# Two more key blocks as 16-bit parts, with their lower halves made by GpSimd

## The chip, the cores and the metric

The kernel runs on one core of a Trainium2 chip. The time is device time in microseconds (us), and the figure compared is the median of several runs. The engines are TensorE (PE, with its weight loads shown apart as PEld), VectorE (DVE), ScalarE (ACT), GpSimd (POOL) and SyncE (SP), which mostly issues DMAs. Each engine works through its own queue in order and waits on semaphores for the others.

## The reference

The input x has 2048 rows of 640 numbers. The result is the sum of x, an attention block and an MLP block, both on the normalised rows:

```
xn = layernorm(x)
q, k, v = split(xn @ wqkv)               # 32 heads of 20 numbers
p = softmax(q @ k.T * 20**-0.5)          # for each head: 2048 x 2048
attention = (p @ v) @ wo
y = layernorm(xn)
mlp = gelu(y @ w1 + b1) @ w2 + b2        # 640 -> 1536 -> 640
out = x + attention + mlp
```

All of it is in 32-bit floats.

## The kernel before, in words

The kernel has three stages. In the first (up to about 236 us) the rows are normalised and transposed, and q, k and v are made. In the last (from about 1272 us) the remaining output projection is done. In between lies the attention stage, and the MLP's matmuls are laid into it as filling.

**The attention loop** (lines 1200 to 1227). It goes over pairs of heads `g`, halves of the queries `hf` and quarters `cc` (512 queries each): 16 x 2 x 2 = 64 accumulations. Each has 16 key blocks `kb` of 128 keys, in four groups of four (`GRP = 4`). For each key block, `scores` (line 742) multiplies two heads' keys and queries into a PSUM tile of 128x1024 (two heads by 512 queries), and ACT writes the exponential of it as 32-bit floats into a tile `p` (line 750). There are seven `p` tiles.

**Split and whole blocks.** The table `SPLIT` (line 27) says how a block enters the second product, p times v. A *whole* block goes into TensorE as 32-bit floats (`vfull`, 32-bit v). A *split* block goes as two 16-bit parts: the upper half of each 32-bit word, read in place as a bfloat16 with a step of two (`upper`, line 753), and the remainder p minus upper, rounded to float16 (`low`, made by DVE on line 762 into a tile of its own, of which there are four). For split blocks v lies as two float16 parts too. Before, `SPLIT` is `(1, 1, 0, 0)` repeated: the first two blocks of each group are split, eight of the 16.

**The second product** (`pv`, line 767) is issued for a whole group at once, one group late: at the last step of the following group. Its results go to one PSUM tile `o`, whose 128 rows are four quarters of 32 (`q`, line 779): a product writes one quarter, so products to different quarters use different columns of the array. A split block has four products with the upper part (two heads by two parts of v, quarters 0 to 3) and two with the lower part; a whole block has two, in 32 bits. The lower products alternate between two quarters of a head:

```
for a in range(2):
    for n, (kb, _, low) in enumerate(split):
        product(2 * a + n % 2, vhalf, of16(kb, a), low[:, a])
```

**The order of a group.** After blocks 0 and 1 of a group have been scored, `rest` (line 757) makes the lower half of block 0, and then a piece of the filling is issued (`other`: MLP or projection matmuls, as many as a running credit of cost allows). After blocks 2 and 3, `rest` is called for the others, and `pv` of the previous group is issued. So DVE has two subtractions per group, one at each step. Beside them DVE does the GELU arithmetic of the MLP (lines 966 to 981), the evictions of the MLP's second layer (line 997) and the normalisation of finished heads (lines 950 to 956).

**GpSimd's queue** in this stage holds only 16 DMAs (line 1051), which add the bias b2 to rows that SP has loaded (line 1050) after SP has stored the rows before (line 1002). After the main loop it makes a selection matrix (line 887).

There is also a path for unusual inputs (`general`, line 1256), which does not run here; it puts the two parts of v together again.

Of the kernel before, what the change touches and what calls it, by code (L numbers as in the profile page):

```python
# [10 lines left out]
F16 = mybir.dt.float16  # L11
# [3 lines left out]
ALU = mybir.AluOpType  # L15
# [3 lines left out]
P = 128  # L19
S, D, H, DH, F = 2048, 640, 32, 20, 1536  # L20
KD = D // P
KF = F // P
NKB = S // P
VW = DH + 1
PAD = 32 - VW
VROW = H * VW + PAD
SPLIT = (1, 1, 0, 0) * (NKB // 4)
NPAIR = H // 2
EPS = 1e-5
TOP = 15.5  # L30
# [3 lines left out]
GRP = 4  # L34
# [10 lines left out]
def mha_mlp_kernel(tc, x, wqkv, wo, w1, b1, w2, b2, out):  # L45
    nc = tc.nc
# [3 lines left out]
    with (  # L50
# [124 lines left out]
        with tc.tile_pool(name="pa", bufs=2) as pa, tc.tile_pool(name="pa1", bufs=1) as pa1, tc.manual_schedule():  # L175
# [33 lines left out]
            for kb in range(NKB):  # L209
                if SPLIT[kb]:  # L210
                    nc.gpsimd.memset(V16[:, kb, :, DH : DH + 1], 1.0)
# [341 lines left out]
            pt = [pts[0][:, 0], pts[0][:, 1], pts[1][:, 0], pts[1][:, 1]]  # L553
# [114 lines left out]
        with ExitStack() as scope:  # L668
# [3 lines left out]
            ptp = pool(name="pt", bufs=2 * GRP - 1)  # L672
# [80 lines left out]
            def upper(pt):  # L753

                return pt.bitcast(BF16).rearrange("p a (n t) -> p a n t", t=2)[:, :, :, 1]

            def rest(unit):

                kb, pt = unit[3:]
                if SPLIT[kb]:  # L760
                    low = ptp.tile([P, 2, 512], F16, tag="low", name="low", bufs=GRP)
                    nc.vector.tensor_sub(low, pt, upper(pt))  # L762
                    unit.append(low)

            evs = {}
# [410 lines left out]
            with tc.manual_schedule():  # L1176
                fill = chain()
                sides.append(fetch_sums())
                credit = 0.0 - next(fill)
                rate = 1.265  # L1180
                groups = [(g, hf, cc, kb) for g, hf in ORDER for cc in range(2) for kb in range(0, NKB, GRP)]
                prev = None

                runs = []

                def other():

                    nonlocal credit
                    if not runs:
                        unit = next(fill)  # L1190
                        if unit is None:
                            credit = 0.0
                            return
                        n, cost = unit
                        k = max(round((cost - credit) / rate) + 1, math.ceil(cost / CHUNK))
                        runs.extend(n * (i + 1) // k - n * i // k for i in range(k))
                    for _ in range(runs.pop(0)):
                        credit -= next(fill)

                for g, hf, cc, kb0 in groups:  # L1200
                    units = []
                    for kb in range(kb0, kb0 + GRP):
                        units.append([g, hf, cc, kb, scores(g, hf, cc, kb)])
                        if kb % 2 == 0:
                            continue
                        reading[0] = kb % GRP > 1 and prev is not None and prev[-1][3] == NKB - 1
                        tick()
                        if kb % GRP == 1:

                            rest(units[0])
                            credit += rate
                            other()
                        else:
                            for u in units[1:]:
                                rest(u)
                            if prev:
                                pv(prev)
                            else:  # L1220

                                credit += rate
                                other()
                    prev = units
                    if cc == 0 and kb0 == 0 and (g, hf) != ORDER[-1]:
                        n = ORDER[ORDER.index((g, hf)) + 1]
                        sides.append(load_stack(*n, *([stacks[g, hf][1]] if n[0] == g else [])))
                n = 0
                reading[0] = False
                ended[0] = True  # L1230
                fetch_results()

                def more(k):
                    nonlocal n
                    for _ in range(k):
                        n += 1
                        cost = next(fill, 0)
                        if isinstance(cost, tuple):
                            cost = next(fill)
                        tick()  # L1240
                        if cost == 0:
                            return False
                    return True

                more(2)
                pv(prev)
                while more(1):
                    pass
                while sides or patient:
                    tick()  # L1250
                flag = nc.values_load(badi, min_val=0, max_val=1)
# [4 lines left out]
def general(tc, nc, V, vscr, qkscr, oscr, accscr, gscale, ident, psS, psO, psM, project):  # L1256


    ds = bass.ds
    nc.sync.dma_start(vscr, V)  # L1260

    assert SPLIT == (1, 1, 0, 0) * (NKB // 4)
    with (
        tc.tile_pool(name="g2", bufs=2) as g2,
        tc.For_i(0, S, P) as t,
    ):
        with tc.For_i(0, D, DH) as r:
            qs = g2.tile([60, P], F16, name="gq")
            ks = g2.tile([60, S], F16, name="gk")
            vr = g2.tile([P, NKB, VW], F32, name="gv")  # L1270
            vt = g2.tile([P, NKB, DH], F32, name="gvt")
            nc.sync.dma_start(qs[: 2 * DH], qkscr[:, ds(r, DH), ds(t, P)])
            nc.sync.dma_start(qs[2 * DH :], qkscr[0, ds(r, DH), ds(t, P)])
            nc.sync.dma_start(ks[:DH], qkscr[0, ds(r + D, DH), :])
            nc.sync.dma_start(ks[DH:], qkscr[:, ds(r + D, DH), :])
            nc.sync.dma_start(vr, vscr[:, :, ds((r // DH) * VW, VW)])
            vp = vr.bitcast(F16)
            for b in range(2):
                nc.vector.tensor_add(vt[:, b::4, :], vp[:, b::4, :DH], vp[:, b::4, VW : VW + DH])
            sf = g2.tile([P, S], F32, tag="sf", name="sf")  # L1280
            m = g2.tile([P, 4], F32, tag="gm", name="gm")
            L = g2.tile([P, 1], F32, tag="gL", name="gL")
            for i in range(2):
                ps = psS.tile([P, 2, 512], F32, tag="s", name="gs")
                for c in range(2):
                    kc = 2 * i + c
                    nc.tensor.matmul(ps[:, c, :], qs, ks[:, kc * 512 : (kc + 1) * 512], start=True, stop=True)
                nc.vector.tensor_copy(sf[:, i * 1024 : (i + 1) * 1024],
                                      ps.rearrange("p a b -> p (a b)"))
            nc.vector.tensor_reduce(m[:, 0:1], sf, AX.X, ALU.max)  # L1290
            nc.vector.tensor_scalar(sf, sf, m[:, 0:1], None, ALU.subtract)
            nc.scalar.activation(sf, sf, AF.Exp, scale=gscale, accum_out=L)
            nc.vector.reciprocal(L, L)
            nc.vector.tensor_scalar(sf, sf, L, None, ALU.mult)
            o = psO.tile([P, 512], F32, tag="o", name="go")
            for kq in range(4):
                pt = psM.tile([P, 512], F32, tag="m", name="gt")
                tt = g2.tile([P, 512], F32, tag="tt", name="tt")
                kb0 = 4 * kq
                for i in range(4):  # L1300
                    nc.tensor.transpose(pt[:, i * P : (i + 1) * P], sf[:, (kb0 + i) * P :][:, :P], ident)
                nc.vector.tensor_copy(tt, pt)
                for i in range(4):
                    nc.tensor.matmul(o[:DH, :P], (vt if SPLIT[kb0 + i] else vr)[:, kb0 + i, :DH], tt[:, i * P : (i + 1) * P],
                                     start=(kb0 + i == 0), stop=(kb0 + i == NKB - 1))
            hl = g2.tile([DH, 2, P], F16, tag="ghl", name="ghl")
            nc.scalar.activation(hl[:, 0], o[:DH, :P], AF.Copy)
            nc.vector.tensor_sub(hl[:, 1], o[:DH, :P], hl[:, 0])
            nc.sync.dma_start(oscr[:, ds(r, DH), ds(t, P)].rearrange("s d t -> d s t"), hl)
        ot = g2.tile([P, KD, 2, P], F16, tag="ot", name="ot")  # L1310
        for s in range(2):
            nc.sync.dma_start(ot[:, :, s, :], oscr[s, :, ds(t, P)].rearrange("(k p) t -> p k t", p=P))
        acc = g2.tile([P, D], F32, tag="acc", name="acc")
        nc.sync.dma_start(acc, accscr[ds(t, P), :])
        project(ot, acc, ds(t, P))
# [27 lines left out]
```

## Time and profile before

| what | value |
|---|---|
| three runs | 1343.22, 1332.72, 1340.56 us (median 1340.56) |
| span of the profiled execution, first to last instruction | 1337.9 us |
| the profiled execution's own time beside its span | not given by the page; the runs lie on both sides of the span |
| mean granted TensorE clock | 0.997 |
| attention stage | about 236 to 1272 us |

The page of the profile gives busy time and its share of the span for each engine, then the chain of work that ended last, then groups of instructions. A group's row reads: line, engine, operation, what it writes and reads, shapes, count; then busy us and the mean length of one in ns; then the engine's idle time just before these instructions and what ended it. A busy share is a mean over the three stages, so the stage that a change touches has to be looked at by itself.

### The profile page before, as it was taken

How to read it: one execution, taken by the hardware profiler on the slowest of the kernel's cores; microseconds unless marked ns; L12 is line 12 of the kernel's file. 1: busy time of each engine (PE TensorE's matmuls, PEld its weight loads, DVE VectorE, ACT ScalarE, POOL GpSimd, SP SyncE). 2: the span in 40 equal slices, each digit the busy share in tenths (PEclk: the TensorE clock that was granted, in tenths of full speed). 3: DMA queues.
4: the chain of work that ended last, by engine and by line, in shares of the span. 5: the costliest groups of instructions: out<-in, count | busy, mean ns of one | idle time of the engine just before them, and what ended most of it. 6: DMA issues, size and time to landing. Idle time of an engine off the chain costs nothing.

```text
span 1337.9 us, 29042 instructions
## 1 busy us (share of the span) xinstructions
PE 1325.8 (99%) x11635; PEld 586.7 (44%) x11635; DVE 1055.1 (79%) x1431; ACT 1128.0 (84%) x1306; POOL 37.5 (3%) x86
## 2 busy tenths in 40 slices
PE   9999899999999999999999999999999999999998
PEld 6645456444434343434343443344443434333366
DVE  7656754998788989878897879888879888997742
ACT  7844334999999999999999999999999999999900
POOL 3010000000000000000000000000000000000000
PEclk9999899999999999999999999999999999999999
DMA  9778723021203232212322132223032323334375
GB/s 279 254 196 176 136 79 104 15 59 39 66 28 103 61 83 81 63 48 59 111 63 81 33 93 66 75 69 94 19 80 71 93 66 87 118 95 118 105 218 188
DMA packets 100326, 129.54 MB, mean 97 GB/s; under 512 B 24292, under 2 KB 66664, under 8 KB 100188
## 3 DMA queue, kind: packets, MB, share of 16 engines
q1 hardware_dynamic: 96652, 120.25, 31.6%
q0 software_dynamic: 2912, 6.90, 2.8%
q8 instruction: 92, 1.51, 0.5%
q10 hardware_dynamic: 624, 0.51, 0.1%
q14 instruction: 46, 0.38, 0.1%
HBM read 82.14 MB, written 42.51 MB: 93 GB/s over the span
## 4 chain that ended last, share of the span: by engine, by line
PE 87%; DVE 6%; DMA 4%; ACT 1%; issue 1%; SPq 0%; ACTq 0%; DVEq 0%
PE o L779 30%; PE s L748 20%; PE py L1061 13%; PE pu L1031 11%; PE z L1146 5%; PE qkp L337 5%; PE vp L410 3%; DVE low L762 2%; DMA xt<-in_A_x_dram 1%; DMA xnt<-row 1%; DMA qkscr<-qkhl 1%; DVE st L255 1%; DVE qkhl L353 1%; ACT p L750 1%; DMA wos<-in_A_wo_dram 0%
## 5 line engine op out<-in xcount | busy, mean ns | idle before, releaser
L750 ACT ACTIVATE p<-s 128x1024 f32<-128x1024 f32 x1024 | 973.9, 1050 | 33.1 <-PE s L748 27.1
L762 DVE TENSOR_TENSOR low<-p 128x1024 f16<-128x1024 f32 x512 | 614.3, 1218 | 144.8 <-ACT p L750 144.0
L779 PE MATMUL o<-p,vfull 128*32 128x512 bf16 (+1 forms) x4096 | 429.0, 493 | 0.0
L748 PE MATMUL s<-qs,ks 61*128 61x512 f16 x2048 | 311.4, 381 | 0.2 <-ACT p L750 0.2
L748 PEld LDWEIGHTS <-ks 61*128 61x128 f16 x2048 | 61.2, 94 | 278.4 <-issue 276.1
L1061 PE MATMUL py<-w2t,hT 128*128 128x320 f16 x1152 | 178.5, 300 | 0.0
L1031 PE MATMUL pu<-xm,w1t 128*128 128x256 f16 x1440 | 178.2, 273 | 0.1
L1031 PEld LDWEIGHTS <-w1t 128*128 128x128 f16 x1440 | 131.0, 98 | 64.0 <-issue 50.2
L1061 PEld LDWEIGHTS <-hT 128*128 128x128 f16 x1152 | 102.3, 98 | 88.1 <-issue 53.9
L337 PE MATMUL qkp<-xnt,wv 128*128 128x512 f16 x600 | 131.1, 379 | 1.3 <-issue 1.3
L779 PEld LDWEIGHTS <-vfull 128*32 128x32 f16 x3072 | 59.9, 95 | 138.4 <-issue 106.9
L779 PE MATMUL o<-low,vfull 128*32 128x512 f16 x1024 | 101.3, 377 | 0.1
L337 PEld LDWEIGHTS <-wv 128*128 128x128 f16 x600 | 58.2, 98 | 71.0 <-issue 1.6
L779 PEld LDWEIGHTS o<-p,vfull 128*32 128x32 f32 x2048 | 61.7, 108 | 53.2
L410 PE MATMUL vp<-wv,xnt 128*128 128x320 f16 x480 | 69.5, 306 | 3.7 <-DVE qkhl L353 3.7
L1146 PE MATMUL z<-w1t,ot 128*128 128x320 f16 x480 | 67.4, 299 | 0.0
L352 ACT ACTIVATE qkhl<-qkp,qks 128x1024 f16<-128x1024 f32 (+1 forms) x24 | 23.1, 964 | 46.3 <-PE qkp L337 26.6
L410 PEld LDWEIGHTS <-xnt 128*128 128x128 f16 x480 | 47.9, 100 | 23.8 <-issue 3.7
L1146 PEld LDWEIGHTS <-ot 128*128 128x128 f16 x480 | 46.0, 98 | 22.9 <-issue 5.5
L353 DVE SCALAR_TENSOR_TENSOR qkhl<-qkp,qks,qkhl 128x1024 f16<-128x1024 f32 (+1 forms) x24 | 26.5, 1104 | 32.9 <-ACT qkhl L352 32.9
L1103 DVE SCALAR_TENSOR_TENSOR acc<-z,sc,acc 128x320 f32<-128x320 f32 x32 | 17.5, 549 | 37.3 <-PE z L1146 37.2
L800 ACT ACTIVATE ev<-o 128x512 f32<-128x512 f32 x64 | 39.5, 618 | 2.2 <-PE o L779 2.1
(195 smaller groups left out, 670.4 us busy)
## 6 DMA issues: line engine op xcount, KB each, us to landing
qkscr<-qkhl SPq DMA_DIRECT2D x40, 256.0 KB
opart<-ev SPq DMA_DIRECT2D x124, 80.0 KB
ks<-qkscr SPq DMA_DIRECT2D x120, 80.0 KB
qs<-qkscr SPq DMA_DIRECT2D x192, 40.0 KB
oa<-opart SPq DMA_DIRECT2D x32, 240.0 KB
xt<-in_A_x_dram SPq DMA_DIRECT2D x16, 320.0 KB
xscr<-xnt SPq DMA_DIRECT2D x4, 1280.0 KB
xm<-xscr SPq DMA_DIRECT2D x8, 640.0 KB
```

Source lines behind the costliest of these rows:

```text
L337: nc.tensor.matmul(ps[:, i, :], wv[:, k, q, a, mm * P : (mm + 1) * P], xnts[c][:, k, b, :], start=(k + n == 0), stop=(k == KD - 1 and n == 2))
L352: nc.scalar.activation(hl[:, 0, i0:i1], ps[:, i0:i1], AF.Copy, scale=a)
L353: nc.vector.scalar_tensor_tensor(hl[:, 1, i0:i1], ps[:, i0:i1], a, hl[:, 0, i0:i1], ALU.mult, ALU.subtract)
L410: nc.tensor.matmul(ps[:, hf, :320], xnts[c][:, k, a, j * P : (j + 1) * P], wv[:, k, 2, b, hf * 320 : (hf + 1) * 320], start=(n == 0), stop ...
L748: nc.tensor.matmul(ps[:, a, :], ks[64 * a : 64 * a + 61, kb * P : (kb + 1) * P], qs[64 * a : 64 * a + 61, cc * 512 : (cc + 1) * 512], star ...
L750: nc.scalar.activation(pt, ps, AF.Exp, scale=QS)
L762: nc.vector.tensor_sub(low, pt, upper(pt))
L779: nc.tensor.matmul(pv.o[32 * q : 32 * q + 32, :], src[:, v0 - PAD * (1 - q % 2) :][:, :32], t, start=q not in pv.begun, stop=last, skip_gr ...
L800: nc.scalar.activation(evs[g, hf][:, cc], pv.o, AF.Copy)
L1031: nc.tensor.matmul(ps[:, i], w1v[:, k, (f + i) // 4, a, fo_ : fo_ + P], xnt[:, k, b, :], start=(n == 0), stop=(n == 3 * KD - 1))
L1061: nc.tensor.matmul(ps[:, :320], hTs[mc][:, f, a, j * P : (j + 1) * P], w2v[:, f, b, hf * 320 : (hf + 1) * 320], start=(n == 0), stop=(n == ...
L1146: nc.tensor.matmul(ps[:, :320], ot[:, k, a, j * P : (j + 1) * P], wov[:, k, b, h * 320 : (h + 1) * 320], start=(n == 0), stop=(n == 3 * KD ...
```

## The change

Ten of the 16 key blocks are split instead of eight. The two more are in the second group of each accumulation (blocks 4 to 7), which becomes wholly split. In that group GpSimd makes the lower halves of blocks 4 and 5, and DVE those of 6 and 7. GpSimd writes in place: the float16 goes into the lower 16 bits of the same 32-bit word of `p`, so no `low` tile is used and the upper halves stay where they are. At the first step of the group both GpSimd subtractions are issued (and the filling), at the second step the two of DVE. The other three groups are as before. Blocks 6 and 7 now have v in two 16-bit parts.

```diff
-SPLIT = (1, 1, 0, 0) * (NKB // 4)
+SPLIT = (1, 1, 0, 0, 1, 1, 1, 1) + (1, 1, 0, 0) * 2
+POOLED = (4, 5)
...
                 kb, pt = unit[3:]
                 if SPLIT[kb]:
-                    low = ptp.tile([P, 2, 512], F16, tag="low", name="low", bufs=GRP)
-                    nc.vector.tensor_sub(low, pt, upper(pt))
+                    if kb in POOLED:
+                        low = pt.bitcast(F16).rearrange("p a (n t) -> p a n t", t=2)[:, :, :, 0]
+                        nc.gpsimd.tensor_tensor(low, pt, upper(pt), ALU.subtract)
+                    else:
+                        low = ptp.tile([P, 2, 512], F16, tag="low", name="low", bufs=GRP)
+                        nc.vector.tensor_sub(low, pt, upper(pt))
                     unit.append(low)
...
-                        if kb % GRP == 1:
-
-
-
+                        if kb in POOLED:
+                            for u in units:
+                                rest(u)
+                            credit += rate
+                            other()
+                        elif kb % GRP == 1:
                             rest(units[0])
                             credit += rate
                             other()
                         else:
-                            for u in units[1:]:
-                                rest(u)
+                            for u in units:
+                                if len(u) == 5:
+                                    rest(u)
```

In `general` the parts of v are put together for every split block instead of every fourth from 0 and from 1.

More of the change, by code (lines that the diff above doesn't have):

```diff
@@ L1260, in general @@
     nc.sync.dma_start(vscr, V)
-    assert SPLIT == (1, 1, 0, 0) * (NKB // 4)
     with (
@@ L1277, in general @@
             vp = vr.bitcast(F16)
-            for b in range(2):
-                nc.vector.tensor_add(vt[:, b::4, :], vp[:, b::4, :DH], vp[:, b::4, VW : VW + DH])
+            for b in range(NKB):
+                if SPLIT[b]:
+                    nc.vector.tensor_add(vt[:, b, :], vp[:, b, :DH], vp[:, b, VW : VW + DH])
             sf = g2.tile([P, S], F32, tag="sf", name="sf")
```

## The prediction

> **What bounds the kernel now.** I read the page first (busy shares, then the chain that ended last), then the busy time of the attention stage by itself, then who waits for whom, and last the order of time on TensorE inside one group of key blocks.
>
> ```profile
> span 1337.9 us, 29042 instructions
> ...
> PE 1325.8 (99%) x11635; PEld 586.7 (44%) x11635; DVE 1055.1 (79%) x1431; ACT 1128.0 (84%) x1306; POOL 37.5 (3%) x86
> ...
> PE 87%; DVE 6%; DMA 4%; ACT 1%; issue 1%; SPq 0%; ACTq 0%; DVEq 0%
> ```
>
> TensorE (PE) is busy 99% of the span and carries 87% of the chain. GpSimd (POOL) does almost nothing. That is a mean over stages, and the change sits only in the attention stage, which the rows of the exp on line 750 place between about 236 and 1272 us. The view of busy time by stretch gives that stage and its tightest 50 us (columns: stretch, length, then busy us and instruction count of PE, PEld, DVE, ACT, POOL; granted clock; DMA share; GB/s):
>
> ```profile
> 236.00:1272.00 1036.00, 1035.59 (x9705) 414.18 (x9697) 885.59 (x1056) 1003.12 (x1125) 13.58 (x16) 1.00 0.26 72
> 250.00:300.00 50.00, 49.76 (x476) 21.41 (x474) 48.49 (x59) 48.78 (x58) 0.00 (x0) 1.00 0.17 47
> ```
>
> So in 1036 us PE has no idle time, ACT has 33 us, and DVE has 150 us (85.5% busy). The stage holds 64 accumulations of 16 key blocks, so one takes 1036 / 64 = 16.19 us, of which DVE works 13.84. The second row shows that DVE can reach 48.49 / 50 = 97% while PE still runs full. Three engines are thus near their limits at once: whoever is given more work has little room. The waits say the same of the order: exp waits for scores, and the subtraction waits for exp.
>
> ```profile
> DVE low L762 <- ACT p L750: 144.0, 121, 8.2
> ...
> ACT p L750 <- PE s L748: 27.1, 110, 0.7
> ```
>
> **What the change takes off TensorE.** Per accumulation two key blocks go from whole (32-bit) to split (16-bit parts). The order of time on PE shows one group with two of each:
>
> ```profile
> 251.10 0.60 PE L748 MATMUL s<-qs,ks 61*128 61x512 f16 x4
> 251.63 0.64 PE L779 MATMUL o<-p,vfull 128*32 128x512 bf16 x8
> 252.10 0.39 PE L779 MATMUL o<-low,vfull 128*32 128x512 f16 x4
> 252.31 1.03 PE L779 MATMUL o<-p,vfull 128*32 128x512 f32 x8
> 253.28 0.60 PE L748 MATMUL s<-qs,ks 61*128 61x512 f16 x4
> ```
>
> From start to start, the split pair takes 252.31 - 251.63 = 0.68 us (0.47 for eight upper products, 0.21 for four lower ones) and the whole pair 253.28 - 252.31 = 0.97. A plain swap saves 0.29 us, times 64 is 18.6 us. But the order of the lower products matters. Each writes a quarter of the array's columns, and the four of a split pair go to quarters 0, 1, 2, 3, which is why they fit into 0.21 us. With four split blocks the loop over a and n issues them to quarters 0, 1, 0, 1, 2, 3, 2, 3. If PE issues in order, that is three rounds of 0.21 and not two, 0.63 against 0.42, and the saving shrinks to 0.29 - 0.21 = 0.08 us, times 64 is 5 us. The busy rows of the three forms over the whole span give the other end:
>
> ```profile
> L779 PE MATMUL o<-p,vfull 128*32 128x512 f32 x2048 | 265.5, 592 | 0.0
> ...
> L779 PE MATMUL o<-p,vfull 128*32 128x512 bf16 x2048 | 163.5, 395 | 0.0
> ...
> L779 PE MATMUL o<-low,vfull 128*32 128x512 f16 x1024 | 101.3, 377 | 0.1
> ```
>
> A split block costs (163.5 + 101.3) / 512 = 0.517 us and a whole one 265.5 / 512 = 0.519, so nothing would be saved; but these modelled ends overlap, and starts are the better measure. Bounds 0 to 18.6 us; I take 5, by the order of the quarters. ACT's work is unchanged.
>
> **What it leaves on DVE.** As many subtractions as before (512): in the second group blocks 6 and 7 take the place of 4 and 5. They come at the second step of the group instead of one in each, so the last of them has about half a group less time before its product. That matters only if DVE is late already.
>
> **What it puts on GpSimd.** 128 subtractions of 128x1024, two operands each, at most two per 16.19 us. No row has one of this size. The nearest are a copy of one operand, a tiny two-operand power, and a fill of one element:
>
> ```profile
> L887 POOL COPY sel<-ident 64x640 f32<-64x640 f32 x2 | 1.4, 710 | 59.0 <-PE o L779 59.0
> ...
> L281 POOL TENSOR_TENSOR r<-ve,nhalf 128x4 f32<-128x4 f32 x4 | 4.2, 1062 | 35.5 <-DVE ve L280 35.5
> ...
> L1330 POOL MEMSET const-float32-0.0<- 128x1 f32 x1 | 0.1, 98 | 0.3 <-issue 0.3
> ```
>
> The copy takes 710 / 640 = 1.11 ns for each element, 1.14 us for 1024. If both operands are fetched at once the subtraction takes 1.14 us; if one after the other, 2.27. I take the second, less the 0.10 us that a fill of one element takes with nothing to move: 2.17 us of data traffic, 128 x 2.17 = 278 us. GpSimd alone has the room for it: 2 x 2.27 = 4.5 us of every 16.19. By the Trainium skill, page GPSIMD Engine Reference, section 3 (Performance versus the Vector engine), a two-input add of 2048 elements takes 4497 ns; half of that is an estimate of 2.25 us, and with it the term would be 288 us; no row here shows it.
>
> **What it does to DVE beside it.** This is the term that decides. The trace has GpSimd's power operation beside two kinds of DVE work:
>
> ```profile
> 53.99 0.82 DVE L422 SCALAR_TENSOR_TENSOR vfull<-vp,vfull 128x640 f16<-128x640 f32 x1
> 54.16 1.01 POOL L281 TENSOR_TENSOR r<-ve,nhalf 128x4 f32<-128x4 f32 x1 [13.87 <-DVE ve L280]
> ...
> 130.09 0.48 DVE L140 CAST w2t<-wtmp 128x640 f16<-128x640 f32 x1
> 130.27 1.20 POOL L263 TENSOR_TENSOR r<-ve,nhalf 128x4 f32<-128x4 f32 x1 [4.80 <-DVE ve L257]
> 130.61 0.83 DVE L141 TENSOR_TENSOR w2t<-wtmp,w2t 128x640 f16<-128x640 f32 x1
> ```
>
> Beside an operation whose large operand is in PSUM the power took 1.01 us. Beside a fast CAST from SBUF to SBUF it took 1.20: it came when the CAST had 130.57 - 130.27 = 0.30 us left, and lost 0.19 of them. So in SBUF the two engines can hold each other up. Against it speaks that the two-operand operation that followed kept its length, 0.83; but by then the power had long read its four elements. Bounds for the subtraction beside DVE: wholly parallel (0 us added) to wholly exclusive (all 278). I take exclusive, for DVE operations with two operands in SBUF, as the nearest row with any conflict goes that way. The Trainium skill, page SBUF — State Buffer, section Who interferes with whom, says that a DVE instruction with two SBUF inputs contends with a GpSimd instruction that reads SBUF, because its second input comes through a read interface that the two share. By that rule the parallel end falls away and the sum would be the one below; of the trace only the CAST rows bear on it, and they agree in direction, with 0.19 us.
>
> Nearly all of DVE's work in the stage is of that kind:
>
> ```profile
> L762 DVE TENSOR_TENSOR low<-p 128x1024 f16<-128x1024 f32 x508 | 609.5, 1218 | 135.3 <-ACT p L750 134.4
> L981 DVE SCALAR_TENSOR_TENSOR hT<-u,sc,hT 128x512 f16<-128x512 f32 x48 | 36.0, 751 | 1.7
> ...
> L966 DVE TENSOR_TENSOR u<-pu,r2f 128x512 f32<-128x512 f32 x47 | 32.1, 683 | 0.1
> L980 DVE TENSOR_SCALAR hT<-u,sc 128x512 f16<-128x512 f32 x48 | 23.4, 487 | 1.7
> L997 DVE SCALAR_TENSOR_TENSOR xb<-py,sc,xb 128x320 f32<-128x320 f32 x32 | 17.4, 544 | 0.0
> ```
>
> Only the last three, 72.9 us or 8% of 885.59, read PSUM or one operand; I let GpSimd run freely beside these, 0.08 x 278 = 22 us.
>
> **The sum.** DVE and GpSimd together need 885.59 + 278 - 22 = 1142 us of a stage that has 1036. If nothing of it stays idle, the stage takes 1142; if 3% stays idle, as in the tightest stretch now, 1142 / 0.97 = 1177. I take the middle, 1160, which is 124 us more. PE's 5 us then buy nothing, because PE waits for lower halves. Span 1337.9 + 124 = 1462. The page gives only the span for its execution; the timed runs lie at 1332.72 to 1343.22 with the median 1340.56, 2.7 above it, so the forecast is 1462 + 2.7, about **1464 us**, 9% slower.
>
> Where the added time would sit: PE and ACT stand still in front of a group's lower products, for a mean of 124 / 64 = 1.9 us in each accumulation.
>
> **What GpSimd's queue adds.** Its 16 loads of the bias (line 1051) stay in the same queue, and each waits for a load on SP that itself waits for a store:
>
> ```profile
> 347.43 0.54 DVE L997 SCALAR_TENSOR_TENSOR xb<-py,sc,xb 128x320 f32<-128x320 f32 x1
> 347.89 1.22 DVE L762 TENSOR_TENSOR low<-p 128x1024 f16<-128x1024 f32 x1
> 348.00 0.37 SPq L1002 DMA_DIRECT2D accscr<-xb  x1
> 350.23 0.36 SPq L1050 DMA_DIRECT2D xb<-in_A_x_dram  x1
> 353.89 0.86 POOL L1051 DMA_DIRECT2D xb<-in_B_b_dram  x1 [48.16 <-DMA xb<-in_A_x_dram]
> ```
>
> From store to bias load 353.89 - 348.00 = 5.9 us. A subtraction that falls behind such a load waits up to that long, and behind it wait the group's lower products. It falls there in 5.9 / 16.19 = 36% of the 16, for 2.9 us on average: 16 x 0.36 x 2.9 = 17 us if nothing covers it, nothing if the distance to the products does (1.5 groups, about 6 us, of which the pair needs 4.5). In the sum I count it as covered, and in the range in full.
>
> **The rivals.** First, on the other side: **the two engines read side by side.** For it speaks the 0.83 us of the operation at 130.61; against it the CAST's 0.19 us. Then DVE stays at 885.59 us, GpSimd's 4.5 us per accumulation fit, and PE's saving counts: 1340.56 - 5 = 1336 us, or 1322 if the lower products overlap after all (18.6 us; ACT's 33 us of idle allow it). It is decided by whether line 762's subtractions keep their 1218 ns and their pace while GpSimd works. Chance 0.13: 0.07 for faster by over 1% (the bound of about 13 us that a measurement of this kernel can tell), 0.06 within.
>
> Second, **GpSimd's latency alone**: side by side, but subtractions stuck behind bias loads. 1340.56 - 5 + about 12 (the 17 us less the 1.5 us of slack in each case) = 1348, within 1%. Chance 0.03.
>
> Third, **exclusive, but with the short subtraction**: 128 x 1.14 = 146, less 8%, gives 885.59 + 146 - 12 = 1020, at 97% 1051, or 15 us more: 1356. This is the low end of the forecast's own case, and already slower by over 1%.
>
> Fourth, exclusive and slower still, because operands in every second 16-bit place cost one more pass: 3 x 1.14 = 3.4 us, 436 us in all, less 8% (35), 1287 / 0.97 = 1326, so about 1631. Chance 0.04.
>
> **How the numbers follow.** The forecast's case has 0.80. Its upper end: no free overlap and the full 2.27 us, (885.59 + 291) / 0.97 = 1213, 177 more, and 17 for the bias loads: 1340.56 + 194 = 1535. I open the range a little, to 1352 and 1545; it leaves out the first two rivals (0.16, most of them below 1352) and the fourth (0.04). Faster 0.07, same 0.06 + 0.03 = 0.09, slower 0.84.
>
> **What the profile of the changed kernel would show.** GpSimd's new row: 128 instructions, 2.2 to 2.3 us each when undisturbed, more if the waiting counts as its own. Line 762 in DVE: longer than 1218 ns on average, or with gaps that end at GpSimd's work. PE with idle time before lower products of the second group, released by DVE's or GpSimd's subtraction, and busy near 90% of the stage instead of 100%. The eight lower products of a split group: 0.63 us from first to last if the rounds are three, 0.42 if two. I would be wrong if line 762 keeps its length and its pace beside GpSimd, or if GpSimd's subtraction takes much less than 1.1 us or more than 3.

## The result and the profile after

The changed kernel takes 1477.04 us (median of four runs, 1471.11 to 1478.59), the kernel before 1338.12 us (four runs, 1332.72 to 1343.22). The ratio is 1.104, with a 95% interval of 1.099 to 1.108: 10% slower. The forecast was 1464 us, in a range of 1352 to 1545.

The page of the changed kernel, its span, busy shares and chain (lines of the code from 760 on have moved down by about five: 762 is now 767, and 764 is GpSimd's subtraction):

```profile
span 1475.9 us, 29806 instructions
...
PE 1379.1 (93%) x11891; PEld 609.1 (41%) x11891; DVE 1202.9 (82%) x1433; ACT 1141.4 (77%) x1306; POOL 334.5 (23%) x216
...
DVE 38%; PE 38%; issue 8%; ACT 7%; DMA 6%; POOL 2%; SPq 1%; DVEq 0%; ACTq 0%; POOLq 0%
```

The chain that was 87% TensorE is now shared between DVE and TensorE. GpSimd itself is only 2% of it, so its own lateness cannot be most of the loss. DVE is busy for 148 us more (1202.9 against 1055.1) with the same number of subtractions. The groups by form show where:

```profile
L767 DVE TENSOR_TENSOR low<-p 128x1024 f16<-128x1024 f32 x512 | 672.4, 1344 | 97.1 <-ACT p L751 96.9
L764 POOL TENSOR_TENSOR p<-p 128x1024 f16<-128x1024 f32 x128 | 297.8, 2355 | 703.1 <-ACT p L751 703.0
...
L784 PE MATMUL o<-low,vfull 128*32 128x512 f16 x1024 | 141.1, 382 | 51.5 <-DVE low L767 50.3
...
L975 DVE TENSOR_TENSOR w<-u 128x512 f32<-128x512 f32 x48 | 52.2, 1087 | 1.6
...
L784 PE MATMUL o<-p,vfull 128*32 128x512 f16 x256 | 48.2, 402 | 16.1 <-POOL p L764 16.1
...
L985 DVE TENSOR_SCALAR hT<-u,sc 128x512 f16<-128x512 f32 x48 | 37.0, 771 | 1.7
L986 DVE SCALAR_TENSOR_TENSOR hT<-u,sc,hT 128x512 f16<-128x512 f32 x48 | 36.0, 751 | 1.7
L971 DVE TENSOR_TENSOR u<-pu,r2f 128x512 f32<-128x512 f32 x48 | 32.8, 683 | 17.0 <-PE pu L1036 16.6
```

The same DVE operations have become longer on average: the subtraction from 1218 to 1344 ns, the square on line 975 (line 970 before, in the row below) from 692 to 1087, the scaling on line 985 from 487 to 771. Line 971, which reads PSUM, kept its 683. TensorE waits 50.3 us for DVE's lower halves, and 16.1 for GpSimd's.

```profile
L970 DVE TENSOR_TENSOR w<-u 128x512 f32<-128x512 f32 x48 | 33.2, 692 | 1.6
```

The order of time shows one such moment whole (POOL, then DVE, then PE):

```profile
303.17 4.19 POOL L764 TENSOR_TENSOR p<-p 128x1024 f16<-128x1024 f32 x2 [15.29 <-ACT p L751]
...
303.27 2.34 DVE L975 TENSOR_TENSOR w<-u 128x512 f32<-128x512 f32 x1
305.54 2.91 DVE L767 TENSOR_TENSOR low<-p 128x1024 f16<-128x1024 f32 x1
308.37 0.68 DVE L977 SCALAR_TENSOR_TENSOR w<-w,u 128x512 f32<-128x512 f32 x1
...
304.64 0.38 PE L784 MATMUL o<-low,vfull 128*32 128x512 f16 x1
308.50 0.61 PE L784 MATMUL o<-low,vfull 128*32 128x512 f16 x3 [3.48 <-DVE low L767]
308.51 2.31 PE L784 MATMUL o<-p,vfull 128*32 128x512 f32 x8
310.76 1.04 PE L749 MATMUL s<-qs,ks 61*128 61x512 f16 x4
```

GpSimd's two subtractions run from 303.17 to 307.36. A square of 0.69 us that starts at 303.27 takes 2.34, and the subtraction behind it ends at 308.45, that is 1.09 us after GpSimd is done: almost its whole length. TensorE waits 3.48 us for it in the middle of a group.

Over the stage, from 236 us to the last exps, the busy times are (the same columns as before: length, then PE, PEld, DVE, ACT, POOL):

```profile
236.00:1409.00 1173.00, 1084.83 (x9910) 433.62 (x9902) 1025.90 (x1051) 1011.98 (x1119) 305.97 (x142) 0.98 0.23 64
```

The stage grew by 137 us (1173 against 1036), and DVE's busy time in it by 140 (1025.90 against 885.59). DVE's idle time stayed: 147 against 150. That is where the added time shows: inside DVE's own instructions.

### The profile page after: what moved, and what is told of

The parts are those of the page before. It is cut to its first block, busy times and chain, and to the rows that moved or that the text cites. A ratio compares the mean times of both kernels' runs of the same rounds, so it can differ in the third digit from the quotient of the medians.

```text
span 1475.9 us, 29806 instructions
## 1 busy us (share of the span) xinstructions
PE 1379.1 (93%) x11891; PEld 609.1 (41%) x11891; DVE 1202.9 (82%) x1433; ACT 1141.4 (77%) x1306; POOL 334.5 (23%) x216
## 4 chain that ended last, share of the span: by engine, by line
DVE 38%; PE 38%; issue 8%; ACT 7%; DMA 6%; POOL 2%; SPq 1%; DVEq 0%; ACTq 0%; POOLq 0%
DVE low L767 18%; PE o L784 10%; PE s L749 7%; PE pu L1036 6%; ACT p L751 5%; PE z L1151 4%; PE py L1066 4%; PE vp L411 3%; PE qkp L338 3%; DVE w L975 2%; DVE hT L985 2%; DVE u L984 2%; DVE u L973 2%; POOL p L764 2%; DVE u L971 2%
## 5 line engine op out<-in xcount | busy, mean ns | idle before, releaser
L767 DVE TENSOR_TENSOR low<-p 128x1024 f16<-128x1024 f32 x512 | 672.4, 1344 | 97.1 <-ACT p L751 96.9
L764 POOL TENSOR_TENSOR p<-p 128x1024 f16<-128x1024 f32 x128 | 297.8, 2355 | 703.1 <-ACT p L751 703.0
L784 PE MATMUL o<-p,vfull 128*32 128x512 bf16 (+2 forms) x4352 | 437.3, 466 | 16.1 <-POOL p L764 16.1
L784 PEld LDWEIGHTS <-vfull 128*32 128x32 f16 x3840 | 90.9, 95 | 269.5 <-issue 216.5
L1036 PE MATMUL pu<-xm,w1t 128*128 128x256 f16 x1440 | 187.0, 282 | 6.7 <-DVE u L971 4.0
L784 PE MATMUL o<-low,vfull 128*32 128x512 f16 x1024 | 141.1, 382 | 51.5 <-DVE low L767 50.3
L784 PEld LDWEIGHTS o<-p,vfull 128*32 128x32 f32 x1536 | 47.6, 109 | 36.2 <-issue 0.6
L984 DVE SCALAR_TENSOR_TENSOR u<-w,u 128x512 f32<-128x512 f32 x48 | 40.0, 834 | 22.6 <-ACT w L982 22.6
L1056 POOL DMA_DIRECT2D xb<-in_B_b_dram x16 | 13.9, 868 | 181.2 <-DVE low L767 71.4
```

The lines of the kernel that those rows point to most:

```text
L764: nc.gpsimd.tensor_tensor(low, pt, upper(pt), ALU.subtract)
L784: nc.tensor.matmul(pv.o[32 * q : 32 * q + 32, :], src[:, v0 - PAD * (1 - q % 2) :][:, :32], t, start=q not in pv.begun, stop=last, skip_gr ...
L984: nc.vector.scalar_tensor_tensor(u, w, 1.0, u, ALU.add, ALU.mult)
L1036: nc.tensor.matmul(ps[:, i], w1v[:, k, (f + i) // 4, a, fo_ : fo_ + P], xnt[:, k, b, :], start=(n == 0), stop=(n == 3 * KD - 1))
```

## The experiments

**Is it GpSimd's work beside DVE, or what it is for?** The kernel before got GpSimd's subtractions as dead weight: two per accumulation into a scratch tile that nobody reads, in pieces that fit its space. `idle_pool` is called at block 5; products and `SPLIT` are those of before.

```diff
+            def idle_pool(units):
+                for u in units:
+                    d = ptp.tile([P, 2, 384], F16, tag="dm", name="dm", bufs=1)
+                    for c0, c1 in ((0, 384), (384, 512)):
+                        nc.gpsimd.tensor_tensor(d[:, :, : c1 - c0], u[4][:, :, c0:c1],
+                                                upper(u[4])[:, :, c0:c1], ALU.subtract)
```

> The kernel before, with GpSimd making the lower halves of blocks 4 and 5 of each accumulation a second time, into a scratch tile that nobody reads (each in two pieces of 768 and 256 elements); DVE and TensorE do what they did before. Theory (GpSimd and DVE exclude each other in SBUF): 128 subtractions of 2.36 us, 302 us, less 22 beside free DVE operations, on DVE's 886 us give 1166 us for a stage that has 1036, at 97 to 100% use 1166 to 1202, so about 1470 us, between 1440 and 1510. Rival one (side by side): 1338, within 10 us. Rival two (the cost is TensorE waiting for GpSimd's results): nobody waits for these, so 1338, within 10 us.

Measured: 1477.56 us, ratio 1.104 (1.099 to 1.109), to within a microsecond the changed kernel's time. GpSimd's pieces and DVE's subtraction:

```profile
L769 POOL TENSOR_TENSOR dm<-p 128x768 f16<-128x768 f32 x128 | 272.3, 2127 | 593.1 <-ACT p L750 588.1
L769 POOL TENSOR_TENSOR dm<-p 128x256 f16<-128x256 f32 x128 | 157.5, 1230 | 10.1
...
L762 DVE TENSOR_TENSOR low<-p 128x1024 f16<-128x1024 f32 x512 | 700.4, 1388 | 110.0 <-ACT p L750 109.1
```

Nothing waits for these results, so neither GpSimd's latency nor the new products are needed for a loss of this size: the work beside DVE is enough. That the two times agree so closely is partly chance. In pieces GpSimd is busy for 430 us here, against 298 in the changed kernel, and DVE's subtraction is longer (1388 against 1344 ns); in the changed kernel, on the other hand, 19 us of the loss go with the bias loads, as the last experiment shows.

With one block instead of two (`for u in units[1:]`):

> As pool_two, but only for block 5: half the GpSimd work. Theory: 886 + 151 - 12 = 1025 us, which just fits into the stage's 1036; at 97% use 1056. So 0 to 25 us more, 1338 to 1365, far less than half of what pool_two costs, because DVE's idle time takes it up. Rival (each GpSimd subtraction costs a fixed time wherever it falls): half of pool_two's cost, about 1405. Side by side: 1338.

Measured: 1373.35 us, ratio 1.025 (1.021 to 1.030). Half the work costs a quarter of the time (35 us of 139), so a fixed price per subtraction is out; DVE's idle time takes up part. The 8 us above the expected 1365 are a miss, taken up below; GpSimd was also busy for 193 us, where 151 had been reckoned.

**Which of GpSimd's work?** A copy (`nc.gpsimd.tensor_copy(d[:, :, : c1 - c0], u[4][:, :, c0:c1])`) in place of the subtraction, and then fills only:

```diff
+                    nc.gpsimd.tensor_copy(d[:, 0, :1], u[4][:, 0, :1])
+                    for _ in range(3):
+                        nc.gpsimd.memset(d, 0.0)
```

> As pool_two, but a copy with one operand in place of the subtraction with two: about 1.14 us per block by the copy row of before. Theory, if the exclusion is by GpSimd's time on the read side, whatever the number of operands: 128 x 1.14 = 146 us, as pool_one, 1338 to 1365. Rival (only GpSimd operations with two operands conflict): 1338 within 7 us, and DVE's subtractions keep 1218 ns.

> As pool_two, but GpSimd only fills the scratch tile with zeros, six fills of 768 elements for each accumulation (after a one-element copy that ties them to the block): some 5 us of GpSimd time without reading SBUF. Theory (it is the reading that conflicts with DVE's second operand): 1338 within 10 us, and line 762 keeps 1218 ns. Rival (GpSimd's being busy at all slows DVE or writes conflict too): 5 us x 64 = 320 us on DVE's 886, 1480 or more.

The copies gave 1375.21 us, ratio 1.028 (1.024 to 1.032), 10 us above the expected range. DVE's subtraction grew to 1290 ns on average, so a single operand read by GpSimd is enough to hold DVE. GpSimd's rows:

```profile
L769 POOL CAST dm<-p 128x768 f16<-128x768 f32 x128 | 180.2, 1408 | 603.5 <-ACT p L750 599.4
L769 POOL CAST dm<-p 128x256 f16<-128x256 f32 x128 | 130.8, 1022 | 8.1
```

That is 311 us of busy records, more than the changed kernel's 298, at a quarter of its cost. So GpSimd's busy time is not the price: a record also holds waiting. The shortest records are 0.83 and 0.40 us for the two pieces, 1.23 us for a block, near the 1.14 expected; those of pool_two are 1.46 and 0.61, 2.07 us for a block. The fills gave 1352.15 us, ratio 1.011 (1.007 to 1.014), a little over the expected 10 us. DVE's rows with the fills:

```profile
L770 POOL MEMSET dm<- 128x768 f16 x384 | 288.7, 752 | 22.4
...
L762 DVE TENSOR_TENSOR low<-p 128x1024 f16<-128x1024 f32 x512 | 614.2, 1218 | 143.6 <-ACT p L750 142.8
...
L987 DVE TENSOR_SCALAR hT<-u,sc 128x512 f16<-128x512 f32 x48 | 32.1, 669 | 1.7
```

With 289 us of fills, as much as the 298 us of subtractions in the changed kernel, DVE's subtraction kept its 1218 ns. So GpSimd's being busy is not the point; its reading is. Of the GELU's operations only the scaling with one operand (line 987 here) became longer, from 487 to 669 ns. It is held by writes too: in the trace every one of its 18 records of 0.89 us and more overlaps a fill. Of the 14 us that the fills cost, 13 are in DVE's busy time from the first exp to the last (907 us against 894), 9 of them that scaling's (48 x 0.18); the rest was not taken apart.

**Which of DVE's work?** First DVE's 512 subtractions were replaced by an operation with one operand, the lower parts of its blocks left out.

```diff
-                        nc.vector.tensor_sub(low, pt, upper(pt))
+                        nc.vector.tensor_scalar(low, upper(pt), 0.0, None, ALU.mult)
```

> The changed kernel, but DVE's 512 lower halves are made by an operation with one operand from SBUF (upper part times zero, read with its step of two) instead of the two-operand subtraction; the lower parts of DVE's blocks are left out of the result. GpSimd's 128 subtractions stay. Theory (the conflict is with DVE's second operand): these no longer wait for GpSimd; only the GELU arithmetic and the normalisation, about 270 us of DVE's time, still do, so most of the 138 us is gone: 1335 to 1375. Rival (GpSimd holds up any DVE work in SBUF): the new operation is about as long as the subtraction (1.1 to 1.2 us), so the time stays at 1440 to 1480.

Measured: 1360.72 us, ratio 1.019 (1.016 to 1.021), inside the range of the theory. It tells little all the same: the operation was much shorter than the subtraction (shortest 621 ns), so DVE was busy with it for some 200 us less, and it was held all the same (up to 4875 ns):

```profile
L767 DVE TENSOR_SCALAR low<-p x512: 621/686/4875, 220.0 to 1292.5; 128x1024 f16<-128x1024 bf16 x171
```

This is a fast form, as the scaling is. So a slow form with one operand was needed, one that gives a minimum beside its output, with a base without GpSimd.

```diff
-                        nc.vector.tensor_sub(low, pt, upper(pt))
+                        tiny = ptp.tile([P, 1], F32, tag="tiny", name="tiny", bufs=4)
+                        nc.vector.tensor_scalar(low, pt, 0.0, None, ALU.mult, ALU.min, accum_out=tiny)
```

> No GpSimd subtractions (blocks 4 and 5 use the lower tiles of 6 and 7, as in no_pool), and DVE's 512 lower halves are made by an operation that reads one operand, the 32-bit p, writes zeros and also gives its minimum to a small tile: a form that is not of the fast kind. The lower parts are left out of the result. This is only the base for one_operand_pool. If the operation takes about as long as the subtraction (1.1 to 1.3 us): 1332 to 1380.

> As one_operand_alone, with GpSimd's 128 subtractions of the changed kernel. Theory (GpSimd's reading conflicts with DVE's second operand, and with fast forms): these 512 operations keep their length beside GpSimd, and only the GELU and normalisation operations, some 30% of DVE's time, still wait; 10 to 50 us more than one_operand_alone. Rival (GpSimd's reading holds up every DVE operation in SBUF): their mean grows as line 767's did, and the time is 100 to 145 us above one_operand_alone.

Measured: 1338.91 us alone (ratio 1.000, 0.998 to 1.002) and 1420.30 with GpSimd (1.060, 1.056 to 1.063). Alone, and then with GpSimd:

```profile
L768 DVE TENSOR_SCALAR_CACHE_REDUCE low<-p 128x1024 f16<-128x1024 f32 x512 | 607.1, 1213 | 106.3 <-ACT p L751 106.0
```

```profile
L768 DVE TENSOR_SCALAR_CACHE_REDUCE low<-p 128x1024 f16<-128x1024 f32 x512 | 606.7, 1212 | 111.2 <-ACT p L751 111.1
L976 DVE TENSOR_TENSOR w<-u 128x512 f32<-128x512 f32 x48 | 50.6, 1054 | 1.6
```

This settles the mechanism. An operation as long as the subtraction, from the same tile, with one operand instead of two, keeps its length (1212 against 1213 ns, longest 1222 in both), while the two-operand square beside it is held as in the changed kernel (1054 ns). The Trainium skill, page SBUF — State Buffer, section Who interferes with whom, says just this: a DVE instruction with two SBUF inputs contends with a GpSimd one that reads, one with at most one SBUF input outside the two-port modes does not. All these runs agree with it. The size was missed: 81 us more than alone, where 10 to 50 were expected. The held time is where it should be (DVE busy 972.5 us in the stage against 892.6, 80 more), but I had set it by these operations' share of DVE's time, and they were held for more than their share.

**What TensorE gains.** GpSimd's subtractions left out, everything else as in the changed kernel; blocks 4 and 5 use the lower tiles of 6 and 7. Then the same with the lower products issued pair by pair.

```diff
-                            for u in units:
-                                rest(u)
                             credit += rate
...
+                            if kb == 7:
+                                units[0].append(units[2][5])
+                                units[1].append(units[3][5])
```

> The changed kernel without GpSimd's subtractions: blocks 4 and 5 use the lower tiles of blocks 6 and 7 in their lower products, so their own lower parts are left out. TensorE issues exactly what the changed kernel issues. It gives TensorE's saving alone. Theory (lower products in three rounds, quarters 0, 1, 0, 1, 2, 3, 2, 3): 5 us less than before, 1333. Rival (two rounds): 18.6 us less, 1320. Rival (the cost sits in the table of split blocks or in the later order of DVE's subtractions, not in GpSimd): 1440 or more.

> As no_pool, with the lower products of the wholly split group issued pair by pair, quarters 0, 1, 2, 3, 0, 1, 2, 3. Theory (in-order issue, two rounds instead of three): 64 x 0.21 = 13 us less than no_pool, 1320, if ACT with its 33 us of idle follows. Rival (TensorE overlaps them in either order): the same as no_pool.

Measured (twelve runs each): 1331.92 us, ratio 0.9986 (0.9974 to 0.9998), and 1332.75 us, ratio 0.9989 (0.9972 to 1.0006). Without GpSimd's subtractions the loss is gone, so it sits neither in the table of split blocks nor in the later place of DVE's subtractions. The saving is some 2 us, and the order makes no difference. On TensorE, two wholly split groups in the order of the change, then one pair by pair:

```profile
300.35 1.09 PE L784 MATMUL o<-p,vfull 128*32 128x512 bf16 x16
301.27 0.60 PE L784 MATMUL o<-low,vfull 128*32 128x512 f16 x8
301.81 0.60 PE L749 MATMUL s<-qs,ks 61*128 61x512 f16 x4
...
316.30 1.09 PE L784 MATMUL o<-p,vfull 128*32 128x512 bf16 x16
317.22 0.73 PE L784 MATMUL o<-low,vfull 128*32 128x512 f16 x8
317.89 0.60 PE L749 MATMUL s<-qs,ks 61*128 61x512 f16 x4
```

```profile
312.69 0.73 PE L784 MATMUL o<-low,vfull 128*32 128x512 f16 x8
313.35 0.61 PE L749 MATMUL s<-qs,ks 61*128 61x512 f16 x4
```

Eight lower products take 0.54 or 0.67 us to the next scores in the one, 0.66 in the other; counted over all 64 such groups of each trace, the median is 0.54 us in both orders. The whole group takes 1.46 us (median) where one with whole blocks takes 1.64, so about 0.18 us are won in each accumulation, 12 us in all on TensorE. The end shows 2 of them: from the first exp to the last TensorE's busy time fell from 1047 to 1041 us, but it is idle for 6 us there instead of 0.4.

**GpSimd or DVE?** All ten lower halves made by DVE, first with one subtraction at the first step of the second group and three at the second (`POOLED = ()`), then two and two, as the changed kernel has them (`if False:` in place of `if kb in POOLED:` in `rest`).

> The changed kernel with all ten lower halves made by DVE, none by GpSimd (at the first step of the second group block 4 only, the other three at the second step; four low tiles as before). Theory: DVE gets 128 x 1.218 = 156 us more, 886 + 156 = 1042 us for a stage of 1036, at 97 to 100% use 1042 to 1074, and waits for low tiles: 1345 to 1385. That would be some 100 us faster than with GpSimd's help, since a GpSimd subtraction takes 2.36 us of DVE's time instead of 1.22. Rival (GpSimd does relieve DVE and something else costs the 138 us): as slow as the changed kernel or slower, 1477 or more.

> As dve_all (no GpSimd, ten lower halves by DVE), but at the places where the changed kernel makes them: blocks 4 and 5 at the first step of the second group, 6 and 7 at the second. Theory A (dve_all's 103 us without DVE work came from its three subtractions at one step): DVE now gets to 97%, 1345 to 1385. Theory B (a stage that DVE bounds leaves about 100 us of idle time on it wherever the work is put, as in the changed kernel, pool_one and pool_copy): 1405 to 1425. In both it is faster than the changed kernel's 1477, which shows that GpSimd's help costs DVE more than the work itself.

Measured: 1422.02 us (ratio 1.065, 1.062 to 1.067) and 1426.21 (1.065, 1.062 to 1.068). Both are some 50 us faster than the changed kernel: help from GpSimd costs more than none. But both are far above the 1345 to 1385 that I expected for DVE at 97% use, and between these two places for the subtractions there is hardly a difference. In the stage, the even version:

```profile
221.00:1356.00 1135.00, 1071.21 (x10072) 434.29 (x10072) 1034.73 (x1193) 1025.02 (x1136) 14.30 (x17) 1.00 0.24 66
```

DVE has 1135 - 1035 = 100 us without work, 9%. The time with neither a DVE nor a GpSimd record, counted in the trace from the first exp to the last, is much the same wherever DVE is overloaded: 96 us in the changed kernel, 100 in pool_two, 99 in pool_one, 103 in dve_all. The trace shows where most of it lies. Two neighbouring accumulations of the even version, each from its first exp to that of the next:

```profile
578.00:595.10 17.10, 16.40 (x157) 6.48 (x155) 16.89 (x20) 16.12 (x19) 0.00 (x0) 1.00 0.13 37
595.10:611.90 16.80, 16.80 (x166) 7.21 (x164) 13.91 (x14) 15.65 (x17) 0.00 (x0) 1.00 0.00 1
```

In the first DVE works for 99% of the time and TensorE has gaps; in the second TensorE has none and DVE is idle for 2.9 us. DVE's work beside the subtractions, the GELU and the normalisation, is spread unevenly. The 32 accumulations with the least of it (3.2 us each on average) hold 78 of the even version's 99 idle us, the 32 with the most (6.9 us) only 21. So DVE bounds some accumulations and TensorE others. This is read from the trace; no run spread that work evenly, and the rest of the idle time stays open.

**GpSimd's queue.** The changed kernel without the 16 bias loads (the line with `accum_op=ALU.add` taken out, so the bias b2 is missing from the result):

> The changed kernel without the 16 bias loads in GpSimd's queue (the bias b2 is left out of the result). Theory (the distance to the products covers them, as the sum counted): 1477, within 5 us. Rival (subtractions stuck behind them stop TensorE): 10 to 17 us less.

Measured: 1457.70 us, ratio 1.088 (1.083 to 1.093): 19 us less than the changed kernel, so the loads are not covered. TensorE's wait for GpSimd's subtractions fell from 16.1 us to

```profile
PE o L784 <- POOL p L764: 4.9, 1, 4.9
```

Part of the 19 us may come from other waits that go with the loads; the same edit on the kernel before was not tried.

## Why the prediction was right

**The deciding term, exclusion, is shown.** The forecast let DVE's two-operand work and GpSimd's subtractions exclude each other. Dead weight alone gives a loss of this size, leaving GpSimd's subtractions out of the changed kernel removes it, one operand fewer on DVE removes the hold from that operation, and fills do not hold the subtraction. The row from which the forecast took exclusion was a poor witness, though: the CAST has one operand and is a fast form, like the scaling, and the one operation there with two operands kept its 0.83 us. The step was right, but that row could not show it.

**The size came out by two misses that cancel, which is luck.** The sum was 1142 us of DVE and GpSimd together, and 0 to 35 us idle, the middle being 1160. Measured in the changed kernel, from the first exp to the last (220 to 1411 us; the same cut is 1048 us in the kernel before, 12 more than the stage of the forecast), are 1191 - 96 = 1095 us with either at work, and 96 with neither. DVE was busy for 151 us more (1041 us from the first exp to the last, against 890 in no_pool), so GpSimd's 298 us held it for about half of their length; 54 lay in DVE's idle time, and 93 beside DVE work that was not held. I had set that free share at 22 us, by operations that read PSUM or one operand, and had not seen that a GpSimd subtraction probably waits for DVE too: its record shows 2355 ns on average, the shortest 1887, which over 128 is 298 against 242 us. And the idle share was set by the tightest 50 us of the kernel before (97%), a stretch dense in DVE's other work: 22 of its 50 us, where the whole stage has 321 of 1036. Three runs that a 97% use was expected of, pool_one and both dve_all, came to about 90%.

**The duration of GpSimd's subtraction** was taken as 2.27 us, 2.17 of it data traffic: two operands one after the other. The shortest record is 1.89 us, the mean 2.36.

**Where the added time sits** was half right. TensorE's idle time in the stage grew from 0.4 to 88 us, 66 of them before lower products, as the forecast had it. But TensorE's busy time grew by 49 us too (1035.6 to 1084.8), which the forecast did not have; the clock, in the last section, is part of it.

**The free operations were partly misnamed.** I counted line 980 (now 985), one operand from SBUF, as free; it went from 487 to 771 ns, and fills hold it too. Lines 966 and 997, which read PSUM, were free as said.

**TensorE's saving** was put at 5 us between bounds of 0 and 18.6. On TensorE itself it is about 12, in the kernel's time about 2. The reason given, three rounds of lower products, is not borne out: the order pair by pair gains nothing, and eight lower products take 0.54 us, neither 0.63 nor 0.42. The 0.1 us above 0.42 may be the time in which the last products run out before the next scores, which was counted as a cost of whole blocks; that was not tested.

**GpSimd's queue** was counted as covered in the sum, with 17 us in the range. Without the loads the kernel is 19 us faster, so the sum should have had it. Most of it is among the 96 us of idle time (79 without the loads), and so among the misses that cancelled.

**The rivals.** Side by side is ruled out by pool_two, and GpSimd's latency alone too. A subtraction of 1.14 us and one of 3.4 us are ruled out by the shortest record, 1.89 us, and the median, 2.33.

## What to carry to other kernels

Before work is moved to an idle engine, look at what the busy neighbour does while it runs: here a GpSimd subtraction beside DVE operations with two SBUF operands took 2.36 us where DVE itself needed 1.22, and DVE was held for about half of that time. Dead weight on the kernel before, with nobody waiting for it, is the cheapest way to tell such a conflict from lateness. And the use that an engine reaches in its tightest stretch is not what it reaches over a whole stage: 97% became some 90% here, most of the idle time being where the engine has less work than on average.

## What was not expected of the hardware

TensorE's granted clock fell from 0.997 to 0.984 on average. It is at half speed for 51 us of the recorded time instead of 11. The rows at 308.51 and 310.76 above show it: after the wait of 3.48 us eight 32-bit products take 2.31 us instead of 1.03 and four scores 1.04 instead of 0.61. So a long wait for a lower half also makes what follows slower. The Trainium skill, page TensorE: Matmul & The Clock Gate, Part 1, says that the clock halves after an idle window of about 3.4 us. This trace agrees only in part: the half speed is recorded from 307.65 on, 2.6 us after TensorE's last product had ended (305.02), and of the ten other stretches at half speed in the stage one follows a wait of over 3.4 us (4.25), while the longest single waits before the rest are 0.8 to 2.5 us. What the lower clock adds to the time was not measured by itself.
